# Pacing the loads of an attention and feed-forward kernel by what has landed

## The chip, the cores and the metric

The kernel runs on one core of one Trainium2 chip. The metric is the device time of one execution in microseconds (us); the time before is the median of three runs. A profile of one execution shows what each engine did: PE multiplies matrices (PEld loads its weights), DVE and ACT work elementwise, POOL here only issues the loads from the main memory, and SP issues the stores and the transposes that the DMA does.

## The reference

Eight sequences of 448 tokens and 12 heads of 64 go through an attention with a squared ReLU in place of the softmax, and then through a gated feed-forward block with an exact GELU. All inputs are float32; the kernel computes in bf16.

```python
# q, k, v: (8, 12, 448, 64)
scores = matmul(q, k.transpose(0, 1, 3, 2)) / sqrt(64)
attn   = maximum(scores, 0) ** 2 / 448
x      = matmul(attn, v)  # heads joined: (3584, 768)
g      = x @ w_gate       # w_gate, w_val: (768, 1536)
out    = (gelu(g) * (x @ w_val)) @ w_out   # w_out: (1536, 768)
```

## The kernel before

The kernel is built from a list of operations with estimated costs. A small planner runs through them at build time, picks the order on each engine, and emits the instructions in that order. PE takes its operations in a fixed order, so a late input stops everything behind it. A load is an operation on POOL; the planner gives it an arrival time from its bytes and a rate.

```python
def load(nbytes, emit, deps=(), cost=0.7, rate=400e3):
    def paced():
        ins = emit()
        for d in deps:
            tc.add_manual_dep(ins.ins, d.ins.name, SYNC, reason="pace")

    op = Op("POOL", cost, paced, deps)
    arrivals[op] = nbytes / rate
    POOL.append(op)
    return op
```

`nbytes` counts the float32 bytes that are read. The planner, for an operation that is a load:

```python
        if op in arrivals:
            dma = max(dma, op.end) + arrivals[op]
            op.lag = dma + 2.0 - op.end
```

The loads come in this order. A load of q or k with four heads reads 0.46 MB, one of v 0.26 MB (and there are two, for the lower and the upper partitions), one of wg or wv 0.79 MB, one of wo 1.18 MB.

```python
    for h0, h1 in ((0, 2), (2, 4), (4, 8), (8, 12)):
        load_qk(0, 0, h0, h1)             # batch 0: loads 1 to 14
        load_qk(0, 1, h0, h1)
        ...
        if h0 > 2:
            load_v(0, h0 - 4, h1 - 4)
    load_v(0, 8, 12)
    load_w12(0)                           # wg and wv of chunk 0: 15, 16
    load_heads(1, 0, 4)                   # batch 1 begins: 17 to 20
    load_w12(1)                           # 21, 22
    load_qk(1, 0, 4, 8)                   # 23
    load_qk(1, 1, 4, 8)                   # 24
    load_w12(2)                           # 25, 26
    load_v(1, 4, 8)                       # 27, 28
    load_qk(1, 0, 8, 12)                  # 29
    load_qk(1, 1, 8, 12)                  # 30
    load_w12(3)                           # 31, 32
    load_v(1, 8, 12)                      # 33, 34
    load_w12(4)                           # 35, 36
    load_w12(5)                           # 37, 38
    for i in range(FC // WOG):
        load_wo(i)                        # 39 to 42

    for m in range(NM - 1):
        for i in range(2):
            load_qk(2, i, 4 * m, 4 * m + 4)   # 43 to 46
```

(The comments with the numbers are added here.) All later loads are given a computation of the batch before as `deps`, after which they may be issued. Four places use the loads that matter below: the q and k of batches 0 and 1 are transposed on PE, those of the later batches are copied by DVE and transposed by the DMA; the gate and value products of feature chunk `fc` need wg and wv of chunk `fc // 2`; the output products of a block of tokens need all four wo, three of the twelve feature chunks from each.

```python
        src = qk16[b].rearrange("p (h c d) -> p h c d", c=SC, d=D)
        for c in range(SC):
            for j in range(2):
                nc.tensor.transpose(t[HALF[j], c, :], src[:, 2 * (2 * m + r) + j, c, :],
                                    ident[:, :], tile_position=(0, P * j))
...
    ops = [[Op(f"PE{r}", GS, lambda r=r, dc=dc: emit(r, dc),
               [w12_op[i][g], x_op[b, dc], *(free if r == 0 and dc == 0 else ())], lag=0.24)
            for dc in range(KC)] for r in range(2)]
...
    ops = [[Op(f"PE{r}", step, lambda r=r, fc=fc: emit(r, fc),
               [wo_op[fc // WOG], *(u_op[b, fc] for b, _ in chunks),
                *(free if r == 0 and fc == 0 else ())], lag=0.24)
            for fc in range(FC)] for r in range(2)]
```

In the first 30 us of the plan, gaps on PE are filled with products of zeros, which keep the engine at work and compute nothing that is used.

Of the kernel before, what the change touches and what calls it, by code (L numbers as in the profile page):

```python
# [88 lines left out]
def kernel(  # L89
# [87 lines left out]
    w12_op, wo_op, head_op = {}, {}, {}  # L177
    qk16, v16 = {}, {}

    def load(nbytes, emit, deps=(), cost=0.7, rate=400e3):  # L180
        def paced():
            ins = emit()
            for d in deps:
                tc.add_manual_dep(ins.ins, d.ins.name, SYNC, reason="pace")

        op = Op("POOL", cost, paced, deps)
        arrivals[op] = nbytes / rate
        POOL.append(op)
        return op

    def load_w12(i):
        cols = slice(i * WCH, (i + 1) * WCH)

        def emit(wt, src):
            return nc.gpsimd.dma_start(
                wt[:, :, :], src[:, cols].rearrange("(c p) f -> p c f", p=128))
        w12_op[i] = [load(4 * d_model * WCH, lambda wt=wt, src=src: emit(wt, src))
                     for wt, src in ((wg[i], moe_w_gate), (wv[i], moe_w_val))]

    def load_wo(i):  # L200
        rows = slice(i * WOG * 128, (i + 1) * WOG * 128)
        wo_op[i] = load(4 * WOG * 128 * d_model, lambda: nc.gpsimd.dma_start(
            wo[i][:, :, :], moe_w_out[rows, :].rearrange("(c p) f -> p c f", p=128)))

    def load_qk(b, i, h0, h1, deps=()):

        src = (q, k)[i]

        def tile_of():
            if b not in qk16:  # L210
                qk16[b] = qkv.tile([128, H * S // P * D], bf16, name="qk16", tag="qk16")
            return qk16[b][HALF[i], :]

        op = load(4 * (h1 - h0) * S * D, lambda: nc.gpsimd.dma_start(  # L214
            tile_of().rearrange("p (h x) -> p h x", h=H)[:, h0:h1, :],
            src[b, h0:h1].rearrange("h (p c) d -> p h (c d)", c=SC)), deps, rate=400e3 if b else 300e3)
        for pr in range(h0 // 2, h1 // 2):
            head_op[b, pr, i] = op
# [579 lines left out]
```

## Time and profile before

| | before |
|---|---|
| time, median of 3 runs | 424.35 us (424.15 to 425.22) |
| span of the profiled execution | 422.0 us |
| PE busy | 415.3 us, 98% |
| ACT busy | 223.9 us, 53% |
| DVE busy | 214.0 us, 51% |
| POOL busy | 73.8 us, 18% |
| read from the main memory | 48.76 MB |

The page cuts the span into 40 slices and gives what the DMA moved in each, in GB/s:

```profile
GB/s 104 190 200 197 200 209 121 137 82 125 89 152 183 91 117 116 157 48 71 145 141 98 44 97 141 139 65 69 122 146 97 40 2 3 50 68 3 2 78 115
```

A slice is 10.55 us. The bytes are counted where they are written, in bf16 for the loads; twice as many are read. The loads that wait for nothing fill the first six slices. The issues of the loads and their times to landing (pieces in KB of bf16):

```profile
v<-in_v_dram POOLq DMA_DIRECT2D x48, 128.0 KB, 4.3
qk<-in_q_dram POOLq DMA_DIRECT2D x23, 224.0 KB, 4.9
qk<-in_k_dram POOLq DMA_DIRECT2D x23, 224.0 KB, 4.8
wg<-in_moe_w_gate_dram POOLq DMA_DIRECT2D x6, 384.0 KB, 10.5
wv<-in_moe_w_val_dram POOLq DMA_DIRECT2D x6, 384.0 KB, 11.4
wo<-in_moe_w_out_dram POOLq DMA_DIRECT2D x4, 576.0 KB, 15.8
```

The last number of a line is the median time from the issue of a load to its landing. A weight load of the first 50 us thus spends most of its time behind others.

### The profile page before, as it was taken

The numbers are of one execution on the slowest core, as the hardware profiler recorded it, in microseconds if no ns is written. First come the engines' busy times: TensorE is split into PE (matmuls) and PEld (weight loads), VectorE is DVE, ScalarE is ACT, GpSimd is POOL, SyncE is SP. The second block draws the span as 40 slices with busy tenths as digits, with TensorE's granted clock in tenths as the row PEclk, the third lists the DMA queues.
The fourth block names the chain that finished last, engine by engine and source line by source line (L and its number), as shares of the span: only waits on it lengthen the run. The fifth ranks groups of instructions, "written<-read, shape, count | busy, mean of one in ns | idle before, by whom it ended". The sixth has DMA issues, their size and how long they took to land.

```text
span 422.0 us, 19608 instructions
## 1 busy us (share of the span) xinstructions
PE 415.3 (98%) x9090; PEld 372.5 (88%) x9090; DVE 214.0 (51%) x347; ACT 223.9 (53%) x320; POOL 73.8 (18%) x120
## 2 busy tenths in 40 slices
PE   8899999999999999999999999999999999999996
PEld 3558778777998999999999889999999989999995
DVE  3876665266655665356543566456643655212201
ACT  5856663377655655555556565565555556222220
POOL 7745400122022131002300122011310000000000
PEclk9999999999999999999999999999999999999999
DMA  7999997779599798635974289635994100220034
GB/s 104 190 200 197 200 209 121 137 82 125 89 152 183 91 117 116 157 48 71 145 141 98 44 97 141 139 65 69 122 146 97 40 2 3 50 68 3 2 78 115
DMA packets 75281, 44.91 MB, mean 106 GB/s; under 512 B 36160, under 2 KB 71744, under 8 KB 75200
## 3 DMA queue, kind: packets, MB, share of 16 engines
q0 software_dynamic: 37152, 24.39, 43.8%
q1 hardware_dynamic: 37888, 19.08, 24.7%
q8 instruction: 71, 1.16, 1.1%
q10 hardware_dynamic: 160, 0.20, 0.1%
q14 instruction: 10, 0.08, 0.1%
HBM read 48.76 MB, written 11.01 MB: 142 GB/s over the span
## 4 chain that ended last, share of the span: by engine, by line
PE 96%; DMA 2%; POOL 1%; issue 0%; ACT 0%; DVE 0%; POOLq 0%
PE ff L162 87%; PE sp L162 8%; DMA qk<-in_k_dram 2%; PE sp L377 1%; POOL qk L214 1%; PE ff L340 1%; PE ff L377 1%; ACT rl L425 0%; DVE osb L613 0%; POOL ident masks.py:199 0%; POOL ident masks.py:197 0%; POOLq L782 0%
## 5 line engine op out<-in xcount | busy, mean ns | idle before, releaser
L425 ACT ACTIVATE rl<-sp 128x896 bf16<-128x896 f32 x168 | 152.4, 918 | 91.2 <-PE sp L162 82.5
L162 PE MATMUL ff<-xT,wg 64*64 64x448 bf16 x2304 | 196.4, 349 | 0.0
L162 PE MATMUL ff<-xT,wv 64*64 64x448 bf16 x2304 | 195.4, 349 | 0.0
L162 PE MATMUL ff<-wo,uT 64*64 64x384 bf16 (+1 forms) x2736 | 151.2, 320 | 0.0
L431 DVE TENSOR_TENSOR attnT<-rl 128x896 bf16<-128x896 bf16 x168 | 104.1, 623 | 68.9 <-ACT rl L425 66.0
L162 PEld LDWEIGHTS <-wv 64*64 64x64 bf16 x2304 | 124.6, 107 | 9.4 <-issue 0.2
L162 PEld LDWEIGHTS <-wg 64*64 64x64 bf16 x2304 | 123.4, 107 | 10.0
L162 PEld LDWEIGHTS <-uT 64*64 64x64 bf16 x2736 | 128.9, 107 | 3.1
L162 PE MATMUL sp<-qkT 64*64 64x448 bf16 (+1 forms) x768 | 107.6, 328 | 0.2 <-ACT rl L425 0.2
L557 DVE TENSOR_TENSOR uT<-gel,ff 128x448 bf16<-128x448 bf16 x96 | 59.6, 621 | 75.1 <-PE ff L162 66.4
L162 PE MATMUL ff<-attnT,v 64*64 64x448 bf16 (+1 forms) x768 | 88.3, 326 | 0.1
L552 ACT ACTIVATE gel<-ff 128x448 bf16<-128x448 f32 x96 | 52.1, 542 | 48.5 <-PE ff L162 48.0
L162 PEld LDWEIGHTS <-qkT 64*64 64x64 bf16 x768 | 46.3, 106 | 9.7 <-issue 3.8
L613 ACT COPY osb<-ff 128x384 f32<-128x384 f32 x54 | 25.8, 477 | 50.2 <-PE ff L162 50.2
L162 PEld LDWEIGHTS <-v 64*64 64x64 bf16 x768 | 47.8, 107 | 3.9 <-issue 1.1
L487 DVE TENSOR_SCALAR xT<-ff 128x448 bf16<-128x448 f32 x48 | 29.9, 624 | 33.0 <-PE ff L162 32.9
L227 POOL DMA_DIRECT2D v<-in_v_dram x48 | 29.6, 622 | 50.4 <-DVE uT L557 32.5
L214 POOL DMA_DIRECT2D qk<-in_q_dram x25 | 15.6, 622 | 112.1 <-DVE uT L557 105.5
L214 POOL DMA_DIRECT2D qk<-in_k_dram x25 | 15.4, 617 | 65.5 <-DVE uT L557 49.3
L262 DVE COPY qkr<-qk 128x1792 bf16<-128x1792 bf16 x18 | 19.4, 1078 | 0.0
L613 DVE COPY osb<-ff 128x192 f32<-128x192 f32 (+1 forms) x3 | 1.2, 421 | 17.9 <-PE ff L162 17.9
L377 PEld LDWEIGHTS <-qk 128*64 128x64 bf16 x168 | 5.1, 109 | 4.0 <-issue 4.0
(23 smaller groups left out, 42.0 us busy)
## 6 DMA issues: line engine op xcount, KB each, us to landing
out_dram<-osb SPq DMA_DIRECT2D x54, 192.0 KB, 3.0
v<-in_v_dram POOLq DMA_DIRECT2D x48, 128.0 KB, 4.3
qk<-in_q_dram POOLq DMA_DIRECT2D x23, 224.0 KB, 4.9
qk<-in_k_dram POOLq DMA_DIRECT2D x23, 224.0 KB, 4.8
wg<-in_moe_w_gate_dram POOLq DMA_DIRECT2D x6, 384.0 KB, 10.5
wv<-in_moe_w_val_dram POOLq DMA_DIRECT2D x6, 384.0 KB, 11.4
wo<-in_moe_w_out_dram POOLq DMA_DIRECT2D x4, 576.0 KB, 15.8
qkT<-qkr SPq DMA_TRANSPOSE x36, 4.6
```

Of the source, the lines that this page charges most:

```text
L162: return nc.tensor.matmul(o, lhsT, rhs, start=start, stop=stop, tile_position=(P * row, P * col))
L214: op = load(4 * (h1 - h0) * S * D, lambda: nc.gpsimd.dma_start(tile_of().rearrange("p (h x) -> p h x", h=H)[:, h0:h1, :], src[b, h0:h1].re ...
L227: return nc.gpsimd.dma_start(v16[b][HALF[i], h0:h1, :, :], v[b, h0:h1].rearrange("h (p c) d -> p h c d", c=SC)[:, :, c0:c0 + VC, :])
L262: nc.vector.tensor_copy(qkr[b][:, m], qk16[b].rearrange("p (h c d) -> p c h d", c=SC, d=D)[:, :, 4 * m:4 * m + 4])
L340: nc.tensor.matmul(t[:, :], warm[:, 0:128], warm[:, :], start=True, stop=True)
L377: nc.tensor.transpose(t[HALF[j], c, :], src[:, 2 * (2 * m + r) + j, c, :], ident[:, :], tile_position=(0, P * j))
L425: nc.scalar.activation(rl[:, :, :], box[0][:, :, 0:S], AF.Relu)
L431: nc.vector.tensor_tensor(a[:, :, :], box[1][:, :, :], box[1][:, :, :], op=ALU.mult)
L487: nc.vector.tensor_scalar_mul(xT[b][:, pr, :], box[0][:, 0:S], scalar1=out_scale)
L552: nc.scalar.activation(gel[b, fc][:, :], box[0][:, 0:S], AF.Gelu)
L557: u_op[b, fc].ins = nc.vector.tensor_tensor(uT[b][:, fc, :], gel.pop((b, fc))[:, :], box[0][:, 0:S], op=ALU.mult).ins
L613: cp.ins = (nc.vector.tensor_copy if last else nc.scalar.copy)(osb[t][:, cols], box[0][:, 0:N]).ins
```

## The change

A load without a `deps` of its own, from the seventeenth on, now waits for an earlier load to land. It is the last one for which the loads behind it, all issued before the new one, come to at most 1.8 MB. So when a load lands, as many are issued as keep about 1.8 MB on their way. The first sixteen, which are the whole first batch and the first chunk of wg and wv, are issued at once as before. The change is meant to keep the queue of the DMA short, so that what is loaded first isn't disturbed by what is needed later.

```diff
+    sent = []
+
+    UNPACED, AHEAD = 16, 1.8e6
+
     def load(nbytes, emit, deps=(), cost=0.7, rate=400e3):
+        if not deps and len(sent) >= UNPACED:
+            ahead, n = 0, len(sent) - 1
+            while ahead + sent[n][1] <= AHEAD:
+                ahead += sent[n][1]
+                n -= 1
+            deps = [sent[n][0]]
+
         def paced():
             ins = emit()
+            op.ins = ins.ins
             for d in deps:
                 tc.add_manual_dep(ins.ins, d.ins.name, SYNC, reason="pace")
 
         op = Op("POOL", cost, paced, deps)
         arrivals[op] = nbytes / rate
         POOL.append(op)
+        sent.append((op, nbytes))
         return op
```

The wait also stands in the planner, as a dependency of the load's operation.

## The prediction

> **What bounds the kernel now.** I read the page's busy table first, then the waits of PE in the first 110 us, then PE's busy time by stretches, and last the load queue on POOL.
>
> ```profile
> PE 415.3 (98%) x9090; PEld 372.5 (88%) x9090; DVE 214.0 (51%) x347; ACT 223.9 (53%) x320; POOL 73.8 (18%) x120
> ...
> PE 96%; DMA 2%; POOL 1%; issue 0%; ACT 0%; DVE 0%; POOLq 0%
> ```
>
> PE is busy for 98% of the span and carries 96% of the chain that ended last. The 2% of DMA in that chain (1.6%, 6.6 us) is one wait for a k load of batch 0, landing at 11.5 us. A busy PE is not yet a full one, so I ask whether it ever waits for a load. The waits of PE from 0 to 110 us, the stretch in which everything that the change touches is loaded and first used:
>
> ```profile
> PE ff L762 <- DVE table L151: 1.2, 1, 1.2
> PE ff L377 <- DMA qk<-in_k_dram: 1.0, 1, 1.0
> PE sp L162 <- ACT rl L425: 0.2, 1, 0.2
> ```
>
> One wait for a load, 1.0 us. It is for the sixth load; the change begins with the seventeenth. The busy time of three stretches (us, PE busy, and last DMA share and GB/s moved):
>
> ```profile
> 30.00:65.00 35.00, 35.00 (x764) 26.97 (x758) 22.48 (x39) 23.60 (x32) 12.35 (x17) 1.00 1.33 202
> 65.00:100.00 35.00, 35.00 (x772) 28.67 (x766) 17.74 (x29) 16.55 (x25) 4.89 (x8) 1.00 0.78 111
> 100.00:360.00 260.00, 260.00 (x5855) 245.46 (x5847) 143.16 (x226) 150.82 (x215) 36.72 (x60) 1.00 0.66 99
> ```
>
> From 30 to 360 us PE has no idle time at all. The reader should see two things. PE starts 21.8 matmuls per us while the loads run at full rate (764/35), and 22.5 when they are few (5855/260), nearly the same with another mix of shapes. And in the first stretch the DMA moves 202 GB/s into SBUF in bf16, which is 404 GB/s read in float32: the load stream is saturated, until about 67 us. So two saturated streams run side by side, and they touch only where a load lands just before its first use.
>
> The load queue before is not free either. On the timeline of POOL:
>
> ```profile
> 22.28 0.62 POOL L214 DMA_DIRECT2D qk<-in_k_dram  x1 [1.52 <-DMA wv<-in_moe_w_val_dram]
> 23.31 0.83 POOL L195 DMA_DIRECT2D wg<-in_moe_w_gate_dram  x1 [0.41 <-DMA qk<-in_q_dram]
> 24.43 0.83 POOL L195 DMA_DIRECT2D wv<-in_moe_w_val_dram  x1 [0.29 <-DMA qk<-in_k_dram]
> ```
>
> From the thirteenth load on POOL waits for landings that no line of the kernel asks for. Numbering the loads, each waits for the one eight before it: number 24 (here at 22.28) for number 16, wv of chunk 0, landed at 13.30 + 8.7 = 22.0. So at most eight loads are on their way, up to about 4.3 MB of float32 (numbers 22 to 29: three weight loads of 0.79 MB, three q or k of 0.46, two v of 0.26). The change lowers a limit that exists already.
>
> **What the Trainium skill says.** "DMA: Bandwidth & Descriptors", section "Anatomy of one DMA": a load issued by GpSimd costs about 2.0 us fixed plus its bytes at 436 GB/s. For a lone q load of 0.46 MB that estimate is 3.05 us; the trace has 3.6 us at 103.51, with data moving, by windows of a quarter us, from 104.75 to 106.5 only. The fixed part agrees, the rate of a lone load is lower. The same page, "Rules for kernel authors", advises to issue early and wait late; pacing goes against that and needs enough bytes behind the awaited load. "SBUF — State Buffer", section on the two sides of SBUF, warns that certain DVE operations lock GpSimd out while it writes descriptors. Whether this lengthens an issue here, the trace before cannot show: the queue hides it.
>
> **The change part by part.** It removes nothing and moves no work. Loads 1 to 16 (all of batch 0, and wg and wv of chunk 0) are as before. Each of the loads 17 to 46 gets one wait, for the last load such that those behind it sum to at most 1.8 MB. Loads after those already wait for a computation and are left alone.
>
> (a) The waits themselves: 30 on POOL, which is busy 18% of the span. They replace the waits for the load eight back, being always stricter. Cost on PE: 0.
>
> (b) Does the DMA run dry? I worked out the awaited load for all 30. Ahead of number 17 are wv and wg, 1.57 MB; of number 18, 1.245; of most weight chunks 1.3 to 1.77; of number 28 and 34, 1.05; of the wo loads 41 and 42, 1.18; the least is 0.92 (number 45, a load of batch 2). At 0.40 MB per us these are 3.9, 3.1, 3.3 to 4.4, 2.6, 2.95 and 2.3 us of work in the queue when the wait ends. Against this stands the loop from landing to the new load's data: from the lone load, 1.25 us from issue to first bytes and 0.6 us from last bytes to landing, 1.85 us in sum, and up to about 2.5 us with the ramp of the first packets. So 2.95 us covers it, 2.6 just does, 2.3 may leave 0.2 us open. Summed over the 26 loads up to the last wo (number 42) I expect the stream to slip by 0 to 1 us, 0.5 in the middle, because sixteen DMA engines do not finish together and the slowest of them sets the landing.
>
> (c) How much slip does PE bear? First use minus landing, both from the trace before. The nearest ones: k of batch 1, second group, 22.28 + 9.9 = 32.2, first transposed at 35.09: 2.9 us. wg of chunk 1, 17.62 + 10.0 = 27.6, first used after the second hidden block, about 32.5: near 5 us; the later chunks 4 to 6. The last wo is the tightest. It lands at 46.45 + 18.7 = 65.15:
>
> ```profile
> wo<-in_moe_w_out_dram POOLq DMA_DIRECT2D x1, 576.0 KB, 18.7
> ```
>
> and the first output block takes its twelve chunks in this order:
>
> ```profile
> 64.36 0.49 PE L162 MATMUL ff<-wo,uT 64*64 64x384 bf16 x4
> ...
> 65.69 0.33 PE L162 MATMUL ff<-wo,uT 64*64 64x384 bf16 x2
> ...
> 66.52 0.49 PE L162 MATMUL ff<-wo,uT 64*64 64x384 bf16 x4
> ```
>
> Two matmuls per chunk; at 65.69 runs chunk 7, at 66.52 chunks 8 and 9, and chunk 9 is the first of the last wo, 66.68. Slack 66.68 - 65.15 = 1.5 us. A slip of 0.5 us is inside it; one of 3 us would stop PE for 1.5 us, and since PE has no idle time until the end, that goes to the total whole. For batch 2's q and k, k lands at 67.3 and the DVE copy that reads it runs at 68.17, followed by 3 us of idle DVE: a slip of up to 4 us is harmless.
>
> (d) The order of the program. It comes from a plan made at build time, with modelled arrivals at 400 GB/s. In it a paced load is issued 2.7 us (2.0 to land, 0.7 to issue) after the awaited one's last byte, so its DMA too stays filled but for numbers 28, 34 and 45 (0.08, 0.08 and 0.4 us). I expect the same order of instructions on PE. Cost 0.
>
> Sum: 0 (waits) + 0.1 (chance of a stall at the last wo, about one in eight for 1 us or so) + 0 (order), and 0.1 of noise upward: 424.35 + 0.2, so 424.6 us.
>
> **The rivals.** First, the shorter queue lets the stream run dry: if each of the some 26 loads lost 0.3 us, the last wo would land 8 us later and PE would stand still for 6, giving 430 to 431 us. For it: the sixteen engines' skew, GpSimd's descriptors perhaps held up by DVE, which is busy 4.84 of 5 us from 20 to 25. Against it: 2.95 us of bytes against a loop of some 2. Second, the change gains: fewer packets in the queue could let batch 0's data land sooner, or PE's instruction fetches pass. For it: PE and ACT are not full before 13 us. Against it: batch 0's loads stand ahead of the paced ones, landings come in the order of issue throughout, and number 17 was issued only at 14.3, after the wait at 11.5 that counts. From 15 to 25 us ACT is busy 9.9 of 10 us and sets the pace. It could give 0.3 to 1 us: 423.4 to 424. Third, a shifted arrival in the plan reorders DVE or ACT near 68 us: within 1 us either way.
>
> **Range and chances.** Nothing saves more than 1 us, so the low end is 423.6. The high end, 426.4, is a slip of about 3.5 us at the last wo. 2% is 8.5 us, which would take a slip of 10 us out of the 42 us from load 17 to the last wo, a rate lower by a fifth: chance 0.03. Faster by 2%: 0.01. Within 2%: 0.96.
>
> **What would show it.** Right: time from issue to landing of wg and wv falls from 10.5 and 11.4 us to about 5, POOL waits for landings a few loads back, the moved GB/s stay near 200 up to 65 us, PE's waits from 30 us on stay empty. Wrong: GB/s of 170 to 190 in that stretch, PE waits for wo, wg or qk after 20 us, or PE's instructions in another order. If the time falls by over 1 us, I overlooked something that the deep queue costs in the first 30 us.

## The result, and the profile after

| | before | changed |
|---|---|---|
| time, median of 6 runs | 424.79 us (423.94 to 427.57) | 437.88 us (433.99 to 439.07) |
| ratio to before, 95% interval | 1 | 1.0285 (1.0236 to 1.0333) |
| span of the profiled execution | 422.0 us | 436.0 us |
| PE busy | 415.3 us | 421.6 us |
| mean clock of PE | 0.998 | 0.985 |

The change makes the kernel slower by 2.85%. The predicted 424.6 us and its range, 423.6 to 426.4, both miss. On the page of the changed kernel, the busy line, the clock and the moved bytes (40 slices of 10.9 us), and the engines of the chain that ended last:

```profile
PE 421.6 (97%) x9087; PEld 373.5 (86%) x9090; DVE 214.0 (49%) x347; ACT 223.8 (51%) x320; POOL 73.8 (17%) x120
...
PEclk9999997799999999999999999999999999999998
...
GB/s 110 185 155 168 147 169 168 112 119 90 110 109 133 176 85 127 126 125 45 102 132 143 62 57 138 124 125 42 113 122 149 39 3 4 39 75 2 3 75 111
...
PE 78%; DMA 18%; POOL 2%; issue 1%; ACT 0%; DVE 0%; POOLq 0%
```

Three things are to be seen. The loads, which moved about 200 GB/s in the first six slices, now move 147 to 169 from the third slice on, and need a seventh. DMA has 18% of the chain where it had 2%. And in the seventh and eighth slices the clock of PE is not full. The same three stretches as before:

```profile
30.00:65.00 35.00, 33.34 (x712) 24.70 (x705) 21.19 (x36) 21.56 (x30) 12.88 (x18) 1.00 1.18 160
65.00:100.00 35.00, 29.66 (x563) 23.51 (x555) 10.52 (x16) 10.78 (x18) 5.71 (x9) 0.85 0.90 136
100.00:360.00 260.00, 258.86 (x5798) 240.35 (x5794) 143.66 (x227) 150.66 (x215) 39.17 (x64) 1.00 0.72 103
```

160 GB/s instead of 202 from 30 to 65 us; then PE idle for 5.3 us of 35, at a mean clock of 0.85. What PE waited for in the whole execution:

```profile
PE ff L162 <- DMA wo<-in_moe_w_out_dram: 5.3, 2, 3.3
...
PE ff L162 <- DMA wg<-in_moe_w_gate_dram: 0.8, 1, 0.8
PE ff L162 <- DMA wv<-in_moe_w_val_dram: 0.7, 1, 0.7
```

**Where the 14 us went.** The two traces can be laid over each other at the GELUs and output copies on ACT, which come in the same order in both. The changed kernel is 0.2 us ahead up to the sixth GELU (46.2 us). Then it falls back in steps: by 1.5 us at the seventh (wg of chunk 3 was late), by 0.9 at the ninth (wv of chunk 4), by 9.6 at the first output copy (the third and fourth wo), and by 2.1 between 142 and 155 us, where one of PE's waits (0.6 us) is for a transpose that the DMA does. The sum is -0.2 + 1.5 + 0.9 + 9.6 + 2.1 = 13.9 us, against a difference of 14.0 between the spans. After 155 us nothing more is lost or won. The last 2.1 us don't belong to the change: the trace of the run with 2.6 MB below loses 2.0 us there too, and its time is that of the kernel before; one of two more profiles of the changed kernel has no such loss.

**Why the loads are late.** One turn of the loop, on the timeline of POOL in the changed kernel:

```profile
30.27 0.83 POOL L208 DMA_DIRECT2D wg<-in_moe_w_gate_dram  x1
31.88 0.83 POOL L208 DMA_DIRECT2D wv<-in_moe_w_val_dram  x1 [0.78 <-DMA wv<-in_moe_w_val_dram]
35.12 0.63 POOL L240 DMA_DIRECT2D v<-in_v_dram  x1 [2.42 <-DMA qk<-in_k_dram]
36.84 0.62 POOL L240 DMA_DIRECT2D v<-in_v_dram  x1 [1.08 <-DMA wg<-in_moe_w_gate_dram]
```

Load 28, the second v, waits for load 25, the wg at 30.27, which takes 6.3 us and lands at 36.57 (its start and the time to landing, rounded to 0.1 us). Behind it are wv and the first v, 1.05 MB, 2.65 us at 0.395 MB per us. If the DMA had just finished wg when it landed, they would last until 39.2, well past the new load's first bytes. The moved bytes in stretches of half a us say otherwise:

```profile
36.50:37.00 0.50, 0.50 (x18) 0.36 (x10) 0.50 (x3) 0.23 (x1) 0.16 (x1) 1.00 1.39 184
37.00:37.50 0.50, 0.50 (x16) 0.50 (x12) 0.50 (x2) 0.46 (x2) 0.50 (x2) 1.00 1.49 217
37.50:38.00 0.50, 0.50 (x18) 0.50 (x13) 0.08 (x1) 0.50 (x1) 0.50 (x1) 1.00 0.69 90
38.00:38.50 0.50, 0.50 (x18) 0.48 (x14) 0.12 (x1) 0.27 (x1) 0.50 (x2) 1.00 0.86 57
38.50:39.00 0.50, 0.50 (x17) 0.50 (x12) 0.50 (x2) 0.14 (x1) 0.18 (x1) 1.00 0.96 120
39.00:39.50 0.50, 0.50 (x19) 0.48 (x13) 0.50 (x2) 0.50 (x1) 0.32 (x1) 1.00 1.44 179
```

The last number falls from 217 to 90 and 57 already 0.9 us after the landing, and is back to 179 only 2.2 us after the issue at 36.84. The queue was shorter than the count of bytes behind the landing suggests, because the landing is reported late.

How late can be worked out. Landings come in the order of issue, so the last byte of load n is moved at about the time at which the bytes of the loads' own DMA queue, summed from the start, reach the sum of loads 1 to n. (The GB/s above also count instruction fetches, some 0.2 MB up to 65 us, so the queue has to be taken alone.) For load 25 that is 35.13: its landing comes 1.4 us later. Over loads 17 to 42 this lag is 1.3 us in the mean in the changed kernel (0.5 to 2.3). For the first four loads, with little in the queue, it is 0.4 to 0.6. And in the kernel before, whose trace I had, it is 1.8 us in the mean (1.4 to 2.7).

The trace also shows what makes the landing late. Sixteen DMA engines share a load, each reports the end of its part by an update of the load's semaphore, and the landing is the last of the sixteen reports. In the kernel before, first and last report of a load lie 2.5 us apart in the mean (2.0 to 3.5, loads 17 to 42), in the changed kernel 1.7 us (0.5 to 3.0), for the first four loads of both 0.2 to 0.4 us. An engine's last packet of a load is four bytes long (there are 1,824, sixteen for each of the 114 loads); from it to the report it takes 0.34 us in the mean over loads 1 to 46 of the changed kernel and 0.35 in the kernel before, 0.33 to 0.34 over the first four. So the report doesn't become slower: the engines drift apart, and those that are ahead run out of bytes while the last one holds back the landing. For the fourth wo of the changed kernel fifteen reports are in at 73.37, the sixteenth at 75.67.

The other end is from the issue to the first packet of a load that finds the queue empty or nearly so: 1.34 us for load 17 and 1.37 for load 43, and until the sixteenth packet 1.83 and 1.58. (The packets of these loads differ in size from those ahead, so their first is known.) From a landing to the issue it takes 0.28 us in most turns, 0.53 to 0.55 in some, and 1.14 before load 40, the second wo, in the kernel before too. So the loop takes about 1.7 + 0.3 + 1.3 to 1.8, that is 3.3 to 3.8 us, and needs 1.3 to 1.5 MB behind the awaited load, more at load 40. The changed kernel has 0.92 to 1.77.

### The profile page after: what moved, and what is told of

The parts are those of the page before. It is cut to its first block, busy times and chain, and to the rows that moved or that the text cites. A ratio compares the mean times of both kernels' runs of the same rounds, so it can differ in the third digit from the quotient of the medians.

```text
span 436.0 us, 19611 instructions
## 1 busy us (share of the span) xinstructions
PE 421.6 (97%) x9087; PEld 373.5 (86%) x9090; DVE 214.0 (49%) x347; ACT 223.8 (51%) x320; POOL 73.8 (17%) x120
## 3 DMA queue, kind: packets, MB, share of 16 engines
q8 instruction: 71, 1.16, 1.1%
## 4 chain that ended last, share of the span: by engine, by line
PE 78%; DMA 18%; POOL 2%; issue 1%; ACT 0%; DVE 0%; POOLq 0%
PE ff L162 73%; DMA wv<-in_moe_w_val_dram 7%; PE sp L162 5%; DMA wo<-in_moe_w_out_dram 3%; DMA qkT<-qkr 3%; DMA wg<-in_moe_w_gate_dram 3%; DMA qk<-in_k_dram 1%; POOL qk L227 1%; POOL v L240 0%; POOL wg L208 0%; ACT rl L438 0%; DVE osb L626 0%; POOL ident masks.py:199 0%; POOL ident masks.py:197 0%; POOLq L208 0%
## 5 line engine op out<-in xcount | busy, mean ns | idle before, releaser
L162 PE MATMUL ff<-wo,uT 64*64 64x384 bf16 (+1 forms) x2736 | 155.1, 325 | 5.3 <-DMA wo<-in_moe_w_out_dram 5.3
L162 PEld LDWEIGHTS <-uT 64*64 64x64 bf16 x2736 | 131.5, 108 | 9.9 <-issue 6.0
L162 PEld LDWEIGHTS <-wv 64*64 64x64 bf16 x2304 | 123.2, 107 | 12.8 <-issue 1.7
L162 PE MATMUL ff<-attnT,v 64*64 64x448 bf16 (+1 forms) x768 | 89.5, 330 | 0.1
L162 PEld LDWEIGHTS <-qkT 64*64 64x64 bf16 x768 | 45.9, 106 | 10.9 <-issue 5.0
```

The costliest lines, as they stand in the source:

```text
L162: return nc.tensor.matmul(o, lhsT, rhs, start=start, stop=stop, tile_position=(P * row, P * col))
```

## The experiments

The theory: (1) the loop under load is longer than what 1.8 MB cover, so the stream dries up at each short turn; PE, which has only 1.5 us of slack at the last wo, stands still; and after a long enough stop its clock is halved for a while. The rivals: (2) the waits themselves, or fewer loads on their way, slow the stream whether it dries up or not; (3) the planner orders the work differently. The built programs speak against (3) from the start: PE, ACT, DVE and SP have the same instructions in the same order as before, buffer numbers left out.

**More and fewer bytes ahead.** Three runs change one number.

```diff
-    UNPACED, AHEAD = 16, 1.8e6
+    UNPACED, AHEAD = 16, 2.6e6     # and 1.2e6, and 2.2e6
```

With 2.6 MB:

> The same 30 waits, with 2.6 MB in place of 1.8. Theory 1 (the loop from the last byte of the awaited load to the first byte of the new one is about 3.85 us under load: 1.8 to landing, 0.25 to the issue, 1.8 to the first byte; 1.54 MB at 0.4 MB per us cover it): at least 1.64 MB now stand behind the awaited load, so the stream does not run dry, moved bytes stay near 200 GB/s, the last wo lands at 65 to 66 us, and the time is 424 to 426 us. Theory 2 (the waits themselves, or the smaller number of loads on their way, slow the stream): still 30 waits, still fewer loads than eight; 430 us or more. Theory 3 (the planner's order): the order is that of the changed kernel, so 434 to 439 us.

With 1.2 MB:

> The same waits with 1.2 MB. Theory 1: with the loop of 3.85 us the last wo slips by some 20 us by load and bytes (lag of 1.8) against 6 to 12 with 1.8 MB; PE waits for wg and wv as well as for wo; the time is 445 to 460 us. Theory 2 (the number of waits costs): as with 1.8 MB, 434 to 439 us. Theory 3 (order): within 1 us of 1.8 MB apart from a few swaps on ACT and DVE.

With 2.2 MB, which ran later:

> The waits at 2.2 MB. Working through the 30 loads with 1.8 us from issue to first byte, 0.25 us from landing to issue and 0.395 MB per us, the last wo slips by 1.3 us with a lag of 1.8 us from last byte to landing, by 2.7 with 2.2 and by 5.2 with 2.7; slack 1.5 us: theory 1 says 425 to 428 us, between the 424.8 of 2.6 MB and the changed kernel. A cause that comes on by steps (the waits as such) would give the 437 us of the changed kernel.

| bytes ahead | time, median | ratio to before (in the same comparison), 95% interval | fourth wo lands (65.15 before) |
|---|---|---|---|
| 2.6 MB | 424.8 us | 1.000 (0.9978 to 1.0023) | 65.3 us |
| 2.2 MB | 428.5 us | 1.0084 (1.0059 to 1.011) | 70.0 us |
| 1.8 MB | 437.88 us | 1.0285 (1.0236 to 1.0333) | 75.6 us |
| 1.2 MB | 445.41 us | 1.0496 (1.0434 to 1.0558) | 84.2 us |

Of the nine runs with 2.2 MB two, 434.2 and 435.37 us at a mean clock of 0.992 and 0.990, count as slow: they are in the median but not in the ratio.

The moved bytes of the run with 2.6 MB, on its page:

```profile
GB/s 103 190 187 196 197 203 146 137 85 122 91 134 202 74 111 124 129 74 71 139 126 115 47 86 138 151 63 69 126 141 99 39 4 3 45 72 3 2 77 114
```

and of the run with 1.2 MB:

```profile
GB/s 107 164 151 124 139 130 144 146 137 114 112 81 148 171 101 118 122 132 63 79 142 137 96 44 112 115 147 44 110 129 136 59 3 4 39 74 1 3 74 110
```

With 2.6 MB all 30 waits are there and PE, ACT, DVE and SP have the same order, and the stream is back at 187 to 203. So neither the waits as such nor the order of the program cost anything: rivals (2) and (3) fall. Nor does a count of loads explain it: at most six are on their way there where before there were eight, and with 2.2 MB and 1.8 MB alike it is five. The loss grows with each step by which the bytes are cut. Working through the 30 loads with a lag of 1.8 us, 0.25 from landing to issue, 1.8 to the first byte and 0.395 MB per us, the fourth wo should slip by 1.3, 5.8 and 19.9 us for 2.2, 1.8 and 1.2 MB; the traces have 4.8, 10.5 and 19.0. The order is right, but the first two slips are 3.5 and 4.7 us larger than the model's, and the 428.5 us of 2.2 MB lie just outside the 425 to 428 expected. The model takes the sixteen engines for one and has one lag and one delay for all loads: the 1.14 us before load 40 are not in it, and with 1.2 MB the lag is 0.9 us in the mean (0.4 to 2.0). What the rest is isn't shown.

**Half of the waits at a time.**

```diff
-        if not deps and len(sent) >= UNPACED:
+        if not deps and UNPACED <= len(sent) < 38:     # loads 17 to 38 alone
```

> The waits of loads 17 to 38 (batch 1 and all wg and wv) stay, those of the four wo and of batch 2 are gone. Theory 1: the slip at load 38 stays near 6 us, and no more is added: the last wo lands 6 us late instead of 10.5, so PE stands still for about 1 us or nothing beyond the 2.3 us that it lost to wg and wv; with less idle time the clock stays high; 428 to 431 us. If instead only the wo waits matter, 425 to 427 us.

```diff
-    UNPACED, AHEAD = 16, 1.8e6
+    UNPACED, AHEAD = 38, 1.8e6                         # loads 39 to 46 alone
```

> Only the waits of loads 39 to 46 (wo and batch 2). Theory 1: 1.18 MB behind the awaited load against the 1.54 needed: 0.9 us of slip for each of loads 40 and 42 or twice that with the longer lag of 2.7 us, so the last wo is 2 to 4 us late, with 1.5 us of slack PE stands still for 0.5 to 2.5 us; 425 to 428 us. If the four wo waits are the whole cause, 434 us or more.

With loads 17 to 38 alone the time is 430.69 us, ratio 1.015 (1.0099 to 1.02); with loads 39 to 46 alone 426.86 us, ratio 1.0062 (1.0043 to 1.0081). PE's waits for loads of the weights in the first of them:

```profile
PE ff L162 <- DMA wo<-in_moe_w_out_dram: 3.2, 2, 1.7
...
PE ff L162 <- DMA wg<-in_moe_w_gate_dram: 0.8, 1, 0.8
...
PE ff L162 <- DMA wv<-in_moe_w_val_dram: 0.2, 1, 0.2
```

The slip at load 38 was 7.4 us, not 6, and PE stood still for longer than expected. Here the wo are not paced, and yet PE waits for them for 3.2 us: the delay is inherited from the loads ahead of them, as one stream carries both. Both halves cost, by 5.9 and 2.1 us against the 424.81 of before beside them. Together 8.0, but the whole change costs 10.8 to 13.1 us in its three measurements (437.88, 436.08 and 436.51 us against 424.79, 424.74 and 425.72). The halves do not add up. One reason may be the clock: in the profiled executions of the halves it is 9 in every slice (8 in the last of one). In two of the four timed runs of loads 17 to 38, 431.09 and 433.69 us, the mean clock was 0.993 and 0.992, so it may have fallen there.

**The clock.** In the changed kernel PE goes idle at 67.96 us for 3.29 us:

```profile
67.61 0.35 PE L162 MATMUL ff<-wo,uT 64*64 64x384 bf16 x2
71.25 0.46 PE L162 MATMUL ff<-wo,uT 64*64 64x384 bf16 x2 [3.29 <-DMA wo<-in_moe_w_out_dram]
...
75.71 0.53 PE L162 MATMUL ff<-wo,uT 64*64 64x384 bf16 x2 [2.06 <-DMA wo<-in_moe_w_out_dram]
```

The same two matmuls take 0.35 us before the stop and 0.53 after the second. In stretches of 4 us, the third number from the right is the clock:

```profile
68.00:72.00 4.00, 0.75 (x10) 0.60 (x11) 0.00 (x0) 0.59 (x1) 0.36 (x2) 0.92 1.13 183
72.00:76.00 4.00, 1.95 (x20) 1.11 (x18) 1.16 (x2) 0.00 (x0) 1.06 (x3) 0.50 0.93 142
76.00:80.00 4.00, 4.00 (x56) 3.27 (x52) 1.69 (x2) 0.00 (x0) 1.18 (x2) 0.50 0.78 114
80.00:84.00 4.00, 4.00 (x86) 3.56 (x82) 0.00 (x0) 0.92 (x2) 0.00 (x0) 0.80 0.42 78
```

From 71.35 to 81.59 us it is 0.50. From 76 to 80 PE starts 56 matmuls, where 4 us at full clock have about 87 (before, 764 in 35 us). The Trainium skill has this in "TensorE: Matmul & The Clock Gate", section "Part 1: The HAM clock gate": after an idle window of about 3.4 us the clock is halved, until a window of 3.4 us has been busy, and the windows run freely. On the way up the trace agrees. In all four executions in which the clock fell (this one, two more of the changed kernel, and the one with 1.2 MB) it was low for 10.24 us, three times 3.41. Counted from the fall, PE was busy for all of the third stretch of 3.41 us in each, and for 2.47, 2.55, 1.13 and 2.74 us of the second. On the way down the trace agrees in part: in the 3.41 us before the fall PE was busy for 0.12, 0.17, 0.84 and, with 1.2 MB, 1.55 us, so a window that is wholly idle wasn't needed. In the run with loads 17 to 38, with stops of 1.5 and 1.7 us in the 4.5 us up to 72.55, it did not fall.

Two runs fill the stop with products of zeros, which compute nothing, so that the clock should stay. The first:

```diff
+            if (t, g, r) == (0, 0, 0) and fc in (6, 9):
+                w = psS[0].tile([128, 2, 512], f32, name="sp", tag="S")
+                for _ in range(16):
+                    nc.tensor.matmul(w[:, 0, :], warm[:, 0:128], warm[:, :], start=True, stop=True)
             for j, (b, c) in enumerate(chunks):
```

> The changed kernel with its waits at 1.8 MB, and on PE sixteen products of zeros (about 3.4 us at full clock) before the first use of the third wo and sixteen before that of the fourth, in the time in which PE would stand still. The landings stay as they are. If the low clock after the idle stretch costs what the trace of the changed kernel suggests (from 75.7 to 81.3 us the clock is 0.5, so half of 5.6 us is lost), the clock stays near 1.0 there and the time falls by 2 to 4 us against the changed kernel, to some 434 us. If the idle time alone is the cost and the low clock is harmless, the time stays at 436 to 439 us.

beside the changed kernel itself:

> The changed kernel once more beside the others of this call: 434 to 439 us, with PE idle for 3 to 6 us before the third and fourth wo, and a clock of 0.5 for about 10 us after it.

435.66 us (ratio 1.0242, 1.021 to 1.0275) against 436.08 (1.0244, 1.0209 to 1.0279): no difference, and not the 2 to 4 us expected. The clock did stay at 1.00. But the second sixteen held chunk 9 until 79.80, while the fourth wo had landed at 78.33, so the remedy cost 1.5 us itself, and in that execution the wo landed 1.6 us later than in the other. The second run has ten products before chunk 6 (the third wo) alone:

> As the run with products of zeros, but only ten of them (2.15 us at full clock), before the first use of the third wo alone, so that they end before it lands and hold up nothing. The clock should stay at 1.0 after it. If the low clock costs what the trace of the changed kernel shows, the first copy of the output comes about 3 us after the fourth wo lands, in place of 5.9 us, and the time is 2 to 3 us below the changed kernel of the same call: about 433.5 to 435 us. If the low clock is harmless, no difference.

beside the changed kernel again:

> The changed kernel beside it: 436 to 438 us, clock of 0.5 for about 10 us, the first copy of the output 5.5 to 6 us after the landing of the fourth wo.

435.26 us (430.63 to 437.05; ratio 1.0212, 1.0166 to 1.0259) against 436.51 (433.99 to 437.31; ratio 1.0245, 1.0208 to 1.0282). The 1.25 us between the medians are less than the spread of either. The ten products did not keep the clock in every run: in the two with a mean clock of 0.998 and 0.999 the time is 430.63 and 433.92 us, in the four with 0.991 to 0.994 it is 434.46 to 437.05 (before, the mean clock is 0.995 to 0.999). The traces are clearer. With the ten products, from 76 to 80 us:

```profile
76.00:80.00 4.00, 4.00 (x106) 3.98 (x101) 1.30 (x2) 0.96 (x2) 0.00 (x0) 1.00 1.01 159
```

106 matmuls instead of 56, and the first output copy at 77.27, 3.1 us after the fourth wo landed (74.18). In the changed kernel beside it the copy comes at 82.70, 5.3 us after the landing (77.39); in the first trace at 81.42, 5.8 us after (75.64). So in a profiled execution the low clock costs 2.2 to 2.7 us. That it does so in every timed run isn't shown.

## Why the prediction was wrong

**The step that failed is (b).** It asked whether the DMA runs dry, and put the loop at "1.25 us from issue to first bytes and 0.6 us from last bytes to landing, 1.85 us in sum, and up to about 2.5 us with the ramp". The question and the sum were the right ones; the terms were mis-sized, because I took both from a lone load at 103.51 us. The first held: 1.3 to 1.4 us, and 1.6 to 1.8 with the ramp. The second is 1.3 to 1.8 us in the mean in the stream, not 0.6, and 0.3 us from the landing to the issue were missing (1.14 at load 40). With 3.3 to 3.8 us in place of 1.85 to 2.5, "2.95 us covers it" turns into a gap of up to about 1 us, again and again: the slip of "0 to 1 us" was 10.5. The list of short turns was incomplete as well: numbers 20 and 40 also have only 1.18 MB behind the awaited load. Step (b) even names what makes the second term long, "sixteen DMA engines do not finish together and the slowest of them sets the landing", but gives it 0.5 us for the whole stream, where it is 1.7 to 2.5 us at each load.

The number was to be had before: the lag under the deep queue stood in the trace of the kernel before. The skill has a remark on load: "DMA: Bandwidth & Descriptors", section "Latency and other measured facts", gives an access to the main memory 0.2 us on average and 2 us at high load, and says that lighter load makes the fixed cost smaller. The lag does grow with load here (0.4 to 0.6 us for the first four loads in both traces, 1.8 in the mean in the stream before), but by the spread of the engines, not by a slower report (0.33 and 0.35 us).

**The first rival was what happened**, a stream that runs dry; I gave it 8 us of slip and 430 to 431 us. It missed a part for which the prediction had no term: the halved clock, about 2.8 us of the 9.6 at wo in the trace. The rest of the 9.6 follows from step (c). The fourth wo landed at 75.64. PE, late by 2.2 us already, would have used it at 66.68 + 2.2 = 68.9, so it lost 6.8; and from the landing to the first output copy 5.8 us passed instead of 3.0.

**Right were** (a), the waits themselves are free (2.6 MB: ratio 1.000); (c), the last wo as the tightest place and the slack of 1.5 us there, and that PE's lost time goes to the total whole; and (d), the order. In (c) I held the slack of 4 to 6 us at the later weights for safe: with 6.4 us of slip at load 38 they too cost time, 2.4 us in all. Of the signs that I named, the times to landing fell to 6.9 and 7.6 us, not to 5, and "GB/s of 170 to 190" as a sign of error was mild: it was 160.

**The second rival**, that a shorter queue helps batch 0, has nothing for it in any trace: the GELUs of the first 46 us come within 0.6 us of before in the changed kernel's three profiles, in no constant direction. The suspicion that DVE holds up the descriptors of POOL's loads isn't borne out by the two loads at which it can be read: to the first packet it took 1.34 us for load 17, with DVE busy for 4.84 of the 5 us from 17 to 22, and 1.37 us for load 43, with DVE busy for 1.16 of the 5 us from 69 to 74.

**Open** is why the sixteen engines drift apart in the stream, and why the one that was last with the fourth wo of the changed kernel came 2.3 us after the other fifteen. No run here tells.

## What to carry to other kernels

A wait for an earlier transfer's landing is a loop: from last byte to landing, to the issue, to the first byte. The bytes left behind the awaited transfer must last for all of it, and its length is to be measured in the stream, by setting each landing against the sum of the bytes that its queue moved, not at a lone transfer. Here, at 0.4 MB per us, 2.6 MB were enough and 2.2 MB were not; and before a saturated stream is slowed at all, ask which consumer has the least slack at its end, for the slip adds up and arrives there.

## What the runs showed of the hardware that was not expected

- A landing comes 0.4 to 0.6 us after the last byte while the queue is short, and 1.4 to 2.7 us after it in a saturated stream (kernel before, loads 17 to 42). The sixteen engines' reports lie 0.3 to 0.4 us apart at the first four loads and 2.0 to 3.5 us in the stream; each report comes about 0.35 us after its engine's last packet in both.
- PE's clock was at 0.50 for 10.24 us in all four executions in which it fell in mid-run, though PE idled for different times meanwhile. It fell after 3.41 us in which PE was busy for 0.12, 0.17, 0.84 and 1.55 us.
- The same kernel's fourth wo landed at 75.6, 76.7 and 77.4 us in three executions; its timed runs spread over 433.99 to 439.55 us. The kernel before, whose PE doesn't wait for these loads, spread over 423.61 to 427.96 us in the same three comparisons.
